# An adaLN transformer block on one core: chunk 1's queries and keys turned by transposing transfers instead of TensorE, with a new fixed order behind the first 150 ranks

## The chip, the core and the metric

The kernel runs on one core of a Trainium2 chip. A core has a tensor engine (PE, with its weight loads PEld shown apart), three engines for element-wise work (VectorE = DVE, ScalarE = ACT, GpSimd = POOL) and a queue engine (SyncE = SP) which here only issues transfers; ACT issues some too. Each engine works through its own list of instructions in order, and waits by semaphores for results of the others. The metric is the device time of one execution in microseconds (us); lower is better. Beside it there is a trace of one profiled execution, whose span runs from the first instruction to the last.

## The reference

One transformer block over S = 2048 tokens of width D = 640, all arrays bf16. The six modulation rows come from `silu(c) @ w_mod`.

```python
h = layernorm(x) * (1 + ca) + sa
q, k, v = split_heads(h @ wqkv)          # 32 heads of 20
scores = q @ k.T * 20 ** -0.5            # mask: 0 <= i - j < 256
x = x + ga * ((softmax(scores) @ v) @ wo)
h = layernorm(x) * (1 + cb) + sb
x = x + gb * ((sigmoid(h @ w_gate) * (h @ w_up)) @ w_down)    # F = 1536
```

A query attends to itself and the 255 tokens before it, so a stretch of 256 queries needs only its own keys and those of the stretch before.

## The kernel before

**Tiling.** The tokens are cut into 8 chunks of 256, each of two blocks of 128. For every chunk the program goes through these stages:

1. Layer norm of the two blocks (statistics on DVE and POOL, `ln_stats`), then turning the normalized rows to hT (D on partitions). For chunks 0 to 2 (`NPH = 3`) PE does this with an identity matrix (`pe_transposes`); later chunks use transposing transfers, `transp_dma` (L801 to L803), followed by the modulation on DVE, ACT or POOL (`modulate`).
2. Projections to Q, K and V (`qkv`, L902), chains of five matmuls L668 of 320 columns in chunk 0 and 480 afterwards, each into one of the four PSUM tiles of pool `p_M`. ACT or DVE copy them out (`evac`, L893 for ACT, L894 for DVE): V into its own tile, Q and K into staging tiles `stg`, in which each head of 20 columns gets 32.
3. Turning Q and K so that the head's columns lie on partitions. This is the place of the change. There are two ways, and `a < NPQ` (L937; a is the chunk) chooses. Either PE does it: two groups (`half`) of four 128x128 matmuls with the identity, M<-ident,stg, into a `p_M` tile, and a copy of 128x512 to QT or KT by ACT or DVE (operations named `qtr` and `evqt`). Or SP issues one transposing transfer of the block from `stg` to QT or KT (`qkt`). Before, `NPQ = 2`, so chunks 0 and 1 go by PE, the rest by transfers.
4. Scores in sets (`score_set`, L669, matmuls of 20 partitions, S<-QT,KT), all into the one large PSUM tile of `p_S`; exp on ACT (L1015, E<-S), which empties it; the masks by POOL selects (L1040). Each half of the heads (q = 0, 1) then has one burst of probability-times-V matmuls (`burst`, L1053, M<-E,V, named `pvs`) into two `p_M` tiles.
5. Normalization on DVE (`norm`): two transposes of 128x512 (L1082), a reciprocal, a multiplication (L1089), a transpose (L1091). The result is written to DRAM (doc) and read back as oT.
6. The output projection with wo and the residual addition, layer norm 2, its transposing transfers and modulation to h2T.
7. The MLP (`mlp`, L1195): gate and up matmuls with wg and wu, 128x256 each, a tanh on ACT (L1209), a product on DVE (L1211, hh), and the down matmuls with wd, followed by the residual addition on DVE (L1230) and the store of the output. The last block of the last chunk is split into columns 320, 192 and 128.

**What sets the order.** The program is first written as a list of some 2,100 operations (`Prog.op`), with their dependences. `PRIO` gives for each operation, in the order of its creation, one number: rank times five plus the number of the engine (PE, ACT, DVE, POOL, SP). `Prog.schedule` goes through the operations by this rank, puts each at the end of its engine's list, and gives PSUM and SBUF tiles their slots; there is no choice of order at run time. The list thus fixes which engine does an operation that several can do (copies, modulations, masks, stores), what precedes what on each engine, and in which order SP issues its transfers.

The one thing before that `schedule` also did was to go through a model of the time (durations, PE's change of mode, a queue of transfers, a port shared by DVE and POOL), only to choose among free slots of a pool the one whose last user was modelled to end first.

In the order before, the first scores of chunk 1 start at 37.23 us, the first MLP matmuls of chunk 0 at 76.8, and chunk 1's first burst at 54.85.

Of the kernel before, what the change touches and what calls it, by code (L numbers as in the profile page):

```python
# [25 lines left out]
SWITCH = 0.095  # L26
ENGATTR = {"pe": "tensor", "act": "scalar", "dve": "vector", "pool": "gpsimd", "sp": "sync"}
ENGS = ("pe", "act", "dve", "pool", "sp")
OVERLAP = {"pe": 0.0, "act": 0.085, "dve": 0.075, "pool": 0.045, "sp": 0.0}
# [52 lines left out]
class Prog:  # L82
# [69 lines left out]
    def schedule(self):  # L152


        free = {e: START for e in ENGS}
        bw = 0.0
        lastturn = False
# [3 lines left out]
        rr = 0  # L161
        pemode = 0
        portend = 0.0
# [16 lines left out]
        for o in sorted(self.ops, key=lambda x: x.prio):  # L180
# [4 lines left out]
            st = max([o.tmin, free[e] + (SWITCH if e == "pe" and o.mode != pemode else 0.0)]  # L185
                     + [d.end + (0.0 if d.eng == "pe" and e == "pe" else d.lat) for d in o.deps])
            if o.isdma and e == "sp":
                st = max(st, bw - QMAX)
            for t in o.tiles:
                if t.slot is None:  # L190
                    step = 1 if t.mate is None else 2
                    best = None
                    for s in range(0, len(t.pool.tenant), step):
                        rts = [slot_time(t.pool, s + k) for k in range(step)]
                        if None not in rts and (best is None or max(rts) < best[0]):
                            best = (max(rts), s)
# [6 lines left out]
                for x in t.prev:  # L203
                    st = max(st, x.end + x.lat)
            if e == "dve" and o.port:
                st = max(st, free["pool"])
            elif e == "pool":
                st = max(st, portend)
            o.start = st
            if e == "pe":  # L210
                pemode = o.mout
            dur = o.dur[e]
            free[e] = st + dur - OVERLAP[e]
            if e == "dve" and o.port:
                portend = free[e]
            if o.isdma:
                turn = o.dlat > 3.0
                if e == "sp" and bw - st > 2.0:
                    free[e] += 0.35 if o.dur[e] > 1.0 else 0.1
                bw = max(st + o.dlat, bw + (MIXED if turn != lastturn and bw > st + o.dlat else 0.0)) + o.work  # L220
                lastturn = turn
                o.end = max(bw - 0.83, st + dur)
                s = rr
                rr = (rr + 1) % NDMA
                dmacnt[s] += 16
                o.key, o.val = f"d{s}", dmacnt[s]
                if dmalast[s] is not None:
                    o.deps.append(dmalast[s])
                dmalast[s] = o
            else:  # L230
                o.end = st + dur
            order[e].append(o)
            o.done = True
            for t in o.tiles:
                t.left -= 1
                if t.left == 0:
                    last = {}
                    for x in t.ops:
                        if x.isdma:
                            last[x] = x  # L240
                    for e2 in ENGS:
                        xs = [x for x in t.ops if x.eng == e2 and not x.isdma]
                        if xs:
                            last[e2] = max(xs, key=lambda x: x.start)
                    t.rel = list(last.values())
                    freed[t] = max(x.end + x.lat for x in t.rel)
        self.order = order
        self.span = max(o.end for o in self.ops)
# [88 lines left out]
def c_pe(n):  # L337
# [3 lines left out]
PE_EPS = 0.14  # L341
PRIO = [
# [117 lines left out]
]  # L460
TR1 = 2
NPH = 3
NPQ = 2
PQ = ()
KEEP = 3
DSAFE = 1.5
# [840 lines left out]
```

## Time and profile before

| | |
|---|---|
| median of 3 runs | 326.33 us (325.88 to 327.26) |
| span of the profiled execution | 324.3 us |
| granted clock of TensorE | 1.000 |
| PE busy | 317.3 us, 98% |
| ACT, DVE, POOL busy | 212.3, 211.8, 187.2 us |
| moved by DMA | 37.85 MB |

The profile gives no time of its own for the profiled execution beside the span; the median of the runs is 2.0 us above that span. In the trace's rows, a group of instructions is written as engine, line, operation, out<-in and shape, with its count. Idle time of an engine stands in brackets with the engine or transfer that ended it. PE's matmuls overlap with their successors, so the length of one (about 0.4 us from issue to end) is more than the time by which it holds PE; that is read from one start to the next.

### The profile page before, as it was taken

Reading aid. Unit: us, or ns where it says so; the run is one execution under the profiler, and the core shown is the slowest. Engines: PE = TensorE matmul, PEld = TensorE weight load, DVE = VectorE, ACT = ScalarE, POOL = GpSimd, SP = SyncE. Lnnn points to the kernel's source line nnn. Section 1 sums busy time; section 2 is a strip of 40 time slices with the busy share of each in tenths; the row PEclk is TensorE's granted clock in tenths of the full one; section 3 lists DMA queues with packets and bytes.
Section 4 is the critical chain, followed back from the end, with each engine's and each line's share of the span. In section 5 each row is a group of like instructions: output and inputs, shape, how many; then the busy total and the mean of one; then the engine's idle time right before and its main releaser. Section 6 shows DMA issues by size and latency. Waiting matters only on the chain.

```text
span 324.3 us, 11594 instructions
## 1 busy us (share of the span) xinstructions
PE 317.3 (98%) x4872; PEld 222.7 (69%) x4873; DVE 211.8 (65%) x424; ACT 212.3 (65%) x316; POOL 187.2 (58%) x276
## 2 busy tenths in 40 slices
PE   8999999989999999999999999999999999999997
PEld 3564545446776568765776467877786788787885
DVE  5797898778687959674477475837463769264332
ACT  1899985889876687788687867786767764011120
POOL 5128869976668694847585939382939691012100
DMA  7998799989891383824405394340213032202101
GB/s 249 371 333 299 165 269 180 200 137 183 260 164 22 83 109 77 152 61 101 85 22 82 97 103 110 92 69 5 81 40 88 3 79 53 76 20 64 40 2 40
DMA packets 71694, 37.85 MB, mean 117 GB/s; under 512 B 45274, under 2 KB 70362, under 8 KB 71642
## 3 DMA queue, kind: packets, MB, share of 16 engines
q1 hardware_dynamic: 69616, 35.31, 48.3%
q10 hardware_dynamic: 2026, 1.80, 2.1%
q8 instruction: 38, 0.62, 0.8%
q14 instruction: 14, 0.11, 0.1%
HBM read 21.30 MB, written 5.25 MB: 82 GB/s over the span
## 4 chain that ended last, share of the span: by engine, by line
PE 73%; DMA 2%; SPq 2%; DVE 1%; POOL 1%; issue 0%; DVEq 0%
PE M L668 61%; PE S L669 6%; PE M L669 5%; DMA gbc<-gate 2%; SPq L803 2%; DVE wd L1192 1%; POOL x L793 0%; POOL st L788 0%; DVE hh L1211 0%; POOL E L1040 0%; DVE x L1230 0%; DVEq L310 0%
## 5 line engine op out<-in xcount | busy, mean ns | idle before, releaser
L1040 POOL TENSOR_SCALAR_AFFINE_SELECT E<-E 128x512 bf16<-128x512 bf16 (+1 forms) x176 | 142.6, 836 | 68.7 <-ACT E L1015 67.0
L1015 ACT ACTIVATE E<-S 128x512 bf16<-128x512 f32 (+2 forms) x184 | 150.9, 878 | 47.4 <-PE S L669 46.5
L668 PE MATMUL M<-wqkv,hT 128*128 128x480 bf16 (+1 forms) x340 | 73.9, 355 | 0.6 <-ACT hT L846 0.5
L668 PE MATMUL M<-h2T,wu 128*128 128x256 bf16 x480 | 68.0, 273 | 0.5 <-DVE hh L1211 0.5
L668 PE MATMUL M<-h2T,wg 128*128 128x256 bf16 x480 | 67.8, 273 | 0.0
L668 PE MATMUL M<-wd,hh 128*128 128x320 bf16 (+2 forms) x396 | 58.1, 295 | 0.0
L1209 ACT ACTIVATE sig<-M 128x512 f32<-128x512 f32 x48 | 28.9, 602 | 44.1 <-PE M L668 41.7
L1211 DVE SCALAR_TENSOR_TENSOR hh<-sig,M 128x512 bf16<-128x512 f32 x48 | 32.4, 681 | 37.1 <-ACT sig L1209 24.0
L668 PEld LDWEIGHTS M<-h2T,wu 128*128 128x128 bf16 x480 | 45.9, 98 | 8.4 <-issue 1.2
L668 PEld LDWEIGHTS M<-h2T,wg 128*128 128x128 bf16 x480 | 45.7, 98 | 7.1
L668 PEld LDWEIGHTS M<-wqkv,hT 128*128 128x128 bf16 x340 | 30.1, 98 | 27.6 <-DMA wqkv<-in_A_wqkv_dram 1.6
L668 PEld LDWEIGHTS M<-wd,hh 128*128 128x128 bf16 x396 | 36.8, 98 | 14.3 <-DVE hh L1211 0.2
L669 PEld LDWEIGHTS S<-QT,KT 20*64 20x64 bf16 (+1 forms) x1856 | 19.9, 100 | 21.3 <-ACT E L1015 12.0
L1230 DVE TENSOR_TENSOR x<-M,x 128x320 bf16<-128x320 f32 (+2 forms) x33 | 15.6, 476 | 27.2 <-PE M L668 27.2
L669 PE MATMUL S<-QT,KT 20*64 20x256 bf16 (+5 forms) x1856 | 32.1, 228 | 1.2 <-ACT E L1015 1.2
L776 DVE BATCH_NORM_STATS2 st<-x 128x6 f32<-128x320 bf16 x64 | 28.6, 477 | 2.3 <-DMA x<-in_A_x_dram 1.9
L1082 DVE STREAM_TRANSPOSE T<-M 128x512 f32<-128x512 f32 x32 | 21.5, 698 | 9.2 <-PE S L669 8.0
L668 PE MATMUL M<-wo,oT 128*128 128x320 bf16 x160 | 25.4, 299 | 0.0
L669 PE MATMUL M<-E,V 128*32 128x128 bf16 (+1 forms) x960 | 22.8, 246 | 0.8 <-ACT E L1015 0.4
L781 POOL TENSOR_SCALAR st<-st 128x2 f32<-128x2 f32 x16 | 3.7, 234 | 33.8 <-DVE st L778 33.6
L669 PEld LDWEIGHTS M<-E,V 128*32 128x32 bf16 x960 | 19.2, 97 | 5.3 <-issue 2.9
L1091 DVE STREAM_TRANSPOSE On<-Tn 128x1024 bf16<-128x1024 bf16 x16 | 19.8, 1240 | 0.3
(77 smaller groups left out, 240.2 us busy)
## 6 DMA issues: line engine op xcount, KB each, us to landing
x<-in_A_x_dram SPq DMA_DIRECT2D x23, 160.0 KB, 2.3
doc<-On SPq DMA_DIRECT2D x56, 40.0 KB
wd<-in_B_w_down_dram SPq DMA_DIRECT2D x4, 480.0 KB
wd<-in_w_mod_dram SPq DMA_DIRECT2D x5, 320.0 KB
wqkv<-in_A_wqkv_dram SPq DMA_DIRECT2D x4, 400.0 KB
wu<-in_w_mod_dram SPq DMA_DIRECT2D x5, 320.0 KB
oT<-doc SPq DMA_DIRECT2D x8, 192.0 KB, 2.5
out_dram<-x SPq DMA_DIRECT2D x9, 160.0 KB
```

Of the source, the lines that this page charges most:

```text
L668: return e.matmul(o, l, r, start=st, stop=sp, skip_group_check=True)
L669: return e.matmul(o, l, r, start=st, stop=sp, tile_position=tp, skip_group_check=True)
L776: A("dve", lambda e, g, bi=bi, j=j: e.bn_stats(v(bi * 12 + j * 6, 6), src[bi].ap[:, j * 320:(j + 1) * 320]), 0.48, reads=[src[bi].r()], wr ...
L781: A("pool", lambda e, g: e.tensor_scalar(v(28, n), var(), EPS, None, op0=ALU.add), 0.2, reads=[st.r(("m", bi)) for bi in range(n)], writes ...
L803: return e.dma_start_transpose(dst(), src())
L1015: A("act", lambda e, eng: e.activation(dst(), src(), ACT.Exp, scale=SM_SCALE), c_act(n), reads=[Sp.r()], writes=[E.r(key)], prio=3, tag=f" ...
L1040: A("pool", lambda e, eng: e.affine_select(rows(dst), rows(src), pattern=[[0, 8], [sign, n]], compare_op=ALU.is_ge, fill=0.0, base=base, c ...
L1082: A("dve", lambda e, g, h=h: e.transpose(T1.ap[:, 512 * h:512 * h + 512], X[h].ap), 0.694, reads=[X[h].r()], writes=[T1.r(h)], prio=3.5, t ...
L1091: A("dve", lambda e, g: e.transpose(On.ap[:], Tn.ap[:]), 1.22, reads=[Tn.r()], writes=[On.r()], prio=4, tag=f"tr2_{a}")
L1209: A("act", lambda e, g, pg=pg, sg=sg: e.activation(sg.ap[:], pg.ap[:], ACT.Tanh, scale=0.5), c_act(512), reads=[pg.r()], writes=[sg.r()], ...
L1211: A("dve", lambda e, g, pu=pu, sg=sg, f0=f0: e.scalar_tensor_tensor(out=hh.ap[:, f0:f0 + 2, :], in0=sg.ap[:].rearrange("p (a b) -> p a b", ...
L1230: A("dve", lambda e, g, ps=ps, bi=bi, c0=c0, n=n: e.tensor_tensor(x1[bi].ap[:, c0:c0 + n], ps.ap[:, 0:n], x1[bi].ap[:, c0:c0 + n], op=ALU. ...
```

## The change

The core is one constant. With `NPQ = 1` chunk 1's four `stg` tiles (Q and K of two blocks) go by a transposing transfer each instead of by eight groups of four matmuls and eight copies. Chunk 0 stays with PE.

```diff
-NPQ = 2
+NPQ = 1
```

With that 16 operations go and 4 come (2,121 to 2,109 in all), and `PRIO` has new numbers. The first 150 ranks keep their operations and engines, apart from two single loads of w_mod columns that change places and one that goes later (SP's list; the other engines' work is the same up to there). Behind them the order is new: projections, score sets, bursts and MLP pieces of neighbouring chunks interleave differently, and 87 operations with a choice of engines change theirs (copies, modulations, masks, stores; POOL gives 18 to DVE and ACT and takes 10, and four output stores go from ACT's queue to SP's). The last chain on PE is no longer the 128 columns of the last block but the second 320 columns of the last chunk's first block. SP's four new transfers stand in the order KT and QT of the second block, QT and KT of the first, ahead of the transfers that turn chunk 3's rows.

`schedule` loses its model of the time. A free slot is chosen by rank: the one whose last user has the lowest rank.

```diff
-        def slot_time(pool, s):
+        def slot_rank(pool, s):
             ten = pool.tenant[s]
             if ten is None:
-                if not all(x.done for x in pool.init[s]):
-                    return None
-                return max([x.end + x.lat for x in pool.init[s]], default=0.0)
+                return -1 if all(x.done for x in pool.init[s]) else None
             return None if ten.left else freed[ten]
...
-        for o in sorted(self.ops, key=lambda x: x.prio):
+        for rank, o in enumerate(sorted(self.ops, key=lambda x: x.prio)):
...
-                        rts = [slot_time(t.pool, s + k) for k in range(step)]
-                        if None not in rts and (best is None or max(rts) < best[0]):
-                            best = (max(rts), s)
+                        ranks = [slot_rank(t.pool, s + k) for k in range(step)]
+                        if None not in ranks and (best is None or max(ranks) < best[0]):
+                            best = (max(ranks), s)
...
                 if t.left == 0:
+                    freed[t] = rank
```

Last, the two `p_M` tiles of a burst need to be neighbours only where one DVE transpose takes both, which it doesn't here (`TR1` is 2):

```diff
     def burst(a, q, Es):
 
         X = [Tile(p_M, f"O{a}_{q}x"), Tile(p_M, f"O{a}_{q}y")]
-        X[0].mate, X[1].mate = X[1], X[0]
+        if TR1 == 1:
+            X[0].mate, X[1].mate = X[1], X[0]
```

More of the change, by code (lines that the diff above doesn't have):

```diff
@@ L25 @@
 NDMA = 24
-SWITCH = 0.095
 ENGATTR = {"pe": "tensor", "act": "scalar", "dve": "vector", "pool": "gpsimd", "sp": "sync"}
 ENGS = ("pe", "act", "dve", "pool", "sp")
-OVERLAP = {"pe": 0.0, "act": 0.085, "dve": 0.075, "pool": 0.045, "sp": 0.0}
 class Res:
@@ L152, in schedule @@
     def schedule(self):
-        free = {e: START for e in ENGS}
-        bw = 0.0
-        lastturn = False
         order = {e: [] for e in ENGS}
@@ L184, in schedule @@
             o.eng = e
[L185 to L188, printed above, removed]
             for t in o.tiles:
@@ L202, in schedule @@
                         take(t.mate, best[1] + 1 - t.odd)
[L203 to L215, printed above, removed]
-            if o.isdma:
[L217 to L223, printed above, removed]
-                rr = (rr + 1) % NDMA
[L225 to L231, printed above, removed]
+            if o.isdma:
+                dmacnt[rr] += 16
+                o.key, o.val = f"d{rr}", dmacnt[rr]
+                if dmalast[rr] is not None:
+                    o.deps.append(dmalast[rr])
+                dmalast[rr] = o
+                rr = (rr + 1) % NDMA
             order[e].append(o)
@@ L236, in schedule @@
                 if t.left == 0:
+                    freed[t] = rank
                     last = {}
[L238 to L244, printed above, removed]
+                    for x in sorted(t.ops, key=lambda x: x.prio):
+                        last[x if x.isdma else x.eng] = x
                     t.rel = list(last.values())
-                    freed[t] = max(x.end + x.lat for x in t.rel)
         self.order = order
-        self.span = max(o.end for o in self.ops)
     def emit(self):
@@ L466 @@
 DSAFE = 1.5
-START = 0.8
-PORTLAG = 0.05
-MIXED = 0.55
 NPB = 0
@@ L484 @@
 WSE = (("dve", "pool"), ("dve", "pool"))
-QMAX = 4.5
 WDT = 72.0
```

3 lines of the change are left out of this document (removed), and 229 rows, old and new, of the table PRIO.

## The prediction

> **What bounds the kernel now.** I read the page's shares of busy time first, then a table of windows that end where TensorE (PE) last waited, then its waits, then the timeline around them.
>
> ```profile
> span 324.3 us, 11594 instructions
> PE 317.3 (98%) x4872; PEld 222.7 (69%) x4873; DVE 211.8 (65%) x424; ACT 212.3 (65%) x316; POOL 187.2 (58%) x276
> PE 73%; DMA 2%; SPq 2%; DVE 1%; POOL 1%; issue 0%; DVEq 0%
> ```
>
> ```profile
> 18.34:37.23 18.89, 18.88 (x244) 11.08 (x240) 16.60 (x38) 16.87 (x30) 12.42 (x18) 1.00 0.81 258
> 37.23:54.85 17.62, 17.10 (x253) 8.24 (x251) 16.00 (x35) 14.38 (x21) 14.39 (x23) 1.00 1.04 222
> 54.85:70.48 15.63, 14.06 (x249) 7.57 (x248) 11.98 (x28) 12.65 (x20) 13.79 (x21) 1.00 1.03 182
> 70.48:86.54 16.06, 15.55 (x282) 11.06 (x283) 12.62 (x23) 13.99 (x23) 11.09 (x14) 1.00 1.01 219
> 86.54:270.02 183.48, 183.46 (x3253) 132.74 (x3254) 119.14 (x225) 135.74 (x191) 125.83 (x169) 1.00 0.41 80
> 270.02:324.30 54.28, 51.89 (x448) 42.86 (x446) 23.73 (x44) 8.45 (x15) 3.65 (x7) 1.00 0.14 40
> ```
>
> The chain that ended last is three quarters PE. The columns of the table are the window, its length, the busy time of PE, PEld, DVE, ACT and POOL, PE's granted clock, DMA share and GB/s. From 86.54 to 270.02 PE works 183.46 of 183.48 us, and in the last window it is idle only in the 2.4 us after its last matmul. So behind 86.54 an order can win nothing: only fewer matmuls or a shorter end count. Between 18.34 and 86.54 PE idles 0.01 + 0.52 + 1.57 + 0.51 = 2.6 us. There no other engine is full either; DVE comes nearest, with 16.00 of 17.62 (91%) in the second window.
>
> ```profile
> 40.48 2.20 PE L668 MATMUL M<-wqkv,hT 128*128 128x480 bf16 x10
> 42.65 0.41 PE L669 MATMUL S<-QT,KT 20*128 20x64 bf16 x32
> ...
> 64.13 0.43 PE L669 MATMUL S<-QT,KT 20*64 20x256 bf16 x24 [0.30 <-ACT E L1015]
> 64.66 2.82 PE L668 MATMUL M<-wqkv,hT 128*128 128x480 bf16 x12
> 67.91 0.43 PE L669 MATMUL S<-QT,KT 20*64 20x256 bf16 x24 [0.42 <-ACT E L1015]
> 68.26 1.79 PE L668 MATMUL M<-wqkv,hT 128*128 128x480 bf16 x8
> 70.48 1.50 PE L669 MATMUL M<-E,V 128*32 128x128 bf16 x64 [0.42 <-ACT E L1015]
> 86.54 1.14 PE L668 MATMUL M<-h2T,wu 128*128 128x256 bf16 x9 [0.51 <-DVE hh L1211]
> ```
>
> The idle column understates a stall. From 40.48 to 42.65 ten projection matmuls pass undisturbed in 2.17 us, 0.217 each. Twelve should take 2.60; from 64.66 to 67.91 they take 3.25, so 0.65 is lost where the column shows 0.42. Measured so, start to start against undisturbed stretches of the same shapes, I find 4.5 us lost between 18.34 and 90, 2.1 of them between 60 and 70.5. Both the score sets and the PV bursts in these rows wait for exps (L1015): a score set may start only when the set before it has left the one PSUM tile p_S.
>
> **The change part by part.**
>
> 1. Eight groups of four transposing matmuls on PE go (chunk 1's Q and K, two blocks, two halves).
>
> ```profile
> 28.18 0.58 PE L668 MATMUL M<-wqkv,hT 128*128 128x480 bf16 x2
> 28.59 0.39 PE L668 MATMUL M<-ident,stg 128*128 128x128 bf16 x4
> 28.82 0.77 PE L668 MATMUL M<-wqkv,hT 128*128 128x480 bf16 x3
> ```
>
> From 28.59 to 28.82 a group holds PE for 0.23 us, so the eight hold it 1.8. They stand before 60 us, in the stretch with stalls, so this is a gain only as far as PE is held by its own work there. All 1.8 at best, nothing if an exp's end sets the time anyway; I take 1.8 and price the stalls in step 3. Nothing else of PE's work changes in number: the rest of the count is equal.
>
> 2. Their evictions go, and four transposing transfers come.
>
> ```profile
> L893 ACT ACTIVATE QT<-M 128x512 bf16<-128x512 f32 x5 | 3.1, 614 | 0.3 <-PE M L668 0.3
> L894 DVE CAST QT<-M 128x512 bf16<-128x512 f32 x3 | 2.1, 686 | 1.1 <-PE M L668 1.1
> L803 SPq DMA_TRANSPOSE KT<-stg x12: 1237/1324/4257, 44.0 to 210.9; - x12
> L803 SPq DMA_TRANSPOSE QT<-stg x12: 1232/1278/2719, 45.6 to 191.2; - x12
> ...
> DMA to landing us min/median/max: 4.0/4.9/5.8
> ```
>
> Six evictions of 0.61 on ACT (3.7 us) and two of 0.69 on DVE (1.4) go, and eight times the wait for a p_M slot. SP issues four transfers more, about 1.3 us each, 5.2 together (17.0 if each takes the longest of its row, 4.26). In the new order they stand in front of hT3's two transfers, the wm2 loads and the gate's transfers; those are used by chunk 3's projections and by the MLP, more than 10 us later, so 5.2 us costs nothing there. At 17 it would reach the chunk 3 projections. By the order the last of the four can go when its staging tile is filled, about 31.3, and SP is free, about 32.0. With the row's 4.0 to 5.8 us it lands at 36.0 to 37.8. PE's program reaches chunk 1's first scores at about 36 (37.23 before), so it costs 0 to 1.8; I take 0.9, the median landing.
>
> The rule that speaks against this: the Trainium skill, "VectorE: DVE Perf Modes", in its section on the three transpose paths, gives 390 ns for a 128x128 bf16 transpose on TensorE and 1309 ns by the DMA crossbar, and advises TensorE wherever PSUM will do as destination. By it a transfer of eight blocks is an estimated 10.5 us and the four in series 42. The trace disagrees on both: eight blocks land within 4.0 to 5.8 us of issue, and four blocks on PE hold it 0.23 us.
>
> 3. The rest of the order is new: the score sets of chunks 1 and 2 start earlier against the projections, eight small jobs leave POOL (modulations, masks, LN applications), ACT loses most, DVE gains. Summing the durations in the new order ahead of chunk 2's second score set (74.44 before, row below) gives PE 47.8 (50.8 before), DVE 47.8 (45.5), ACT 42.0 (46.7), POOL 42.6 (44.8).
>
> ```profile
> L1015 ACT ACTIVATE E<-S 128x512 bf16<-128x512 f32 x120 | 67.3, 602 | 29.4 <-PE S L669 29.0
> ```
> ```profile
> 54.85 0.85 PE L669 MATMUL M<-E,V 128*32 128x128 bf16 x32
> ...
> 74.44 0.41 PE L669 MATMUL S<-QT,KT 20*128 20x64 bf16 x32
> ```
>
> Walking through the new order with these durations, I get: the first chunk-1 score set at about 36.5; the fourth held about 0.9 us by four exps of 0.60 in a row; first PV burst of chunk 1 about 51.5 to 52 (54.85 before); its second about 67 (70.48); chunk 2's second set 71.1 to 72. Some of each lead is only PE work moved behind the point. The stalls by 90 us add up to 3.4 with the first scores on time and 4.2 with them 0.9 late. I take 3.7 against 4.5: -0.8. Ends: 1.0 (the exps of the new order find p_S free earlier throughout) and 7.6 (DVE sets the pace, below).
>
> 4. The end. In the old order the last chain is the narrow one:
>
> ```profile
> 320.62 0.49 DVE L1230 TENSOR_TENSOR x<-M,x 128x320 bf16<-128x320 f32 x1 [1.47 <-PE M L668]
> 321.95 0.29 DVE L1230 TENSOR_TENSOR x<-M,x 128x128 bf16<-128x128 f32 x1 [0.31 <-PE M L668]
> ```
> ```profile
> x<-in_A_x_dram SPq DMA_DIRECT2D x23, 160.0 KB, 2.3
> out_dram<-x SPq DMA_DIRECT2D x1, 48.0 KB, 1.5
> ```
>
> In the new one PE ends with the first block's second 320 columns, followed by an addition of 0.49 instead of 0.29 and a store of the whole 160 KB. The addition costs 0.2; the store between 0 and 0.8 (2.3 for a 160 KB load against 1.5), I take 0.3: together +0.5.
>
> Four of the output stores move from ACT to SP and two x loads exchange queues late in the run; both queues have room in the fifth window (DMA share 0.41), so nothing, or 0.4 us of PE if an x arrives late. X tiles of a burst are no longer adjacent, which with two separate transposes (L1082) changes no instruction; 0.
>
> **Sum.** The profile gives the execution's span, 324.3; the median of the three runs (326.33, from 325.88 to 327.26) is 2.0 above it, and I take these 2.0 as what lies around the span in either kernel. 324.3 + 2.0 = 326.3; 326.3 - 1.8 (PE work) - 0.8 (stalls) + 0.5 (end) = 324.2.
>
> **The rivals.**
>
> *The order gains more.* Stalls fall to about 1.5: 326.3 - 1.8 - 3.0 + 0.5 = 322.0, with 1.0 and no cost at the end 321.0. For it: ACT and POOL have 4.7 and 2.2 us less to do by 74 us. Against: the single p_S remains, and the four-exp groups with it.
>
> ```profile
> PE S L669 <- ACT E L1015: 1.2, 4, 0.4
> ```
>
> *PE's saved work becomes idle.* If the exps set the pace up to 70 us, the 1.8 us are waited out: stalls 5 to 6.5, 325.0 to 326.5. For it: the longest list of PE's waits in this stretch is on L1015 (the row above). Against: they come to 1.2 us by that column, and ACT is only 81 to 89% busy in those windows.
>
> *DVE becomes the bound (the other side).* 47.8 us of DVE from 18.34 until chunk 2's second set: at 91%, the best window above, it takes 52.5 us and fits the walk. At 85.5%, its mean over the first three windows (44.58 of 52.14), it takes 55.9, 3.1 more, and the time is 324.2 + 3.1 = 327.3; at 84% 328.3. It decides from 87% down, where the 2.1 us gained are spent. For it: DVE carries evictions of projections, turned O and modulations on which PE's slots depend. Against: part of its 85.5% was waiting for PE.
>
> *The transfers come late (also slower).* If the four are issued at the longest in the row and land at 5.8, the last lands at 32.0 + 4.3 + 5.8 = 42.1 instead of 36.9, and since PE's order is fixed all 5.2 count: 329.4. It decides where the landing comes after 39, 7 us behind the issue. For it: DMA share 1.04 at 37 to 55 us, and wm loads in the same window. Against: twelve such transfers never took over 5.8. The skill's advice for TensorE points this way, though by its own figure the time would be far longer.
>
> **How the numbers follow.** A measurement here tells about 0.5% from no change (1.6 us: 324.7 to 328.0). Chances: the forecast, 323.3 to 325.1, 0.38 (0.28 of it under 324.7); the larger gain 0.20; idle instead of work 0.17; DVE 0.17 (half under 328.0); late transfers 0.08 (all slower). Faster 0.28 + 0.20 = 0.48, slower 0.08 + 0.08 = 0.16, same the other 0.36. The range from 321.0 to 328.3 leaves out the late transfers and the tail of the DVE case, and a little below. The forecast's own range is 323.3 to 325.1.
>
> **What would show it.** Right: 32 matmuls M<-ident,stg fewer; QT and KT transfers x14 each on SP, the first ones landing before PE's first 64-row score set, which starts at 36 to 38 without a wait for QT or KT; PE's lost time by 90 us about 3.7; PE gapless behind; a DVE addition 128x320 as the last one. Wrong: a wait of PE on stg's turned tiles, DVE over 90% busy in 40 to 75 us with waits <-DVE in PE's list, or PE idle behind 90 us, which no step here foresees.

## The result, and the profile after

The changed kernel takes 328.63 us (median of 6 runs, 327.27 to 330.03) where the kernel before took 326.11 beside it (6 runs, 325.86 to 327.26): ratio 1.0075, 95% interval 1.0055 to 1.0096. It is 2.5 us slower; 324.2 had been forecast. (The ratios here and below leave disturbed executions out, the medians do not; the two differ by up to 0.13 per cent.) The times also spread more: 2.8 us from lowest to highest, against 1.4.

The page of the kernel after, its span, its shares and its chain:

```profile
span 327.0 us, 11522 instructions
PE 315.2 (96%) x4840; PEld 220.3 (67%) x4841; DVE 210.4 (64%) x424; ACT 213.4 (65%) x316; POOL 181.0 (55%) x268
PE 81%; DVE 3%; DMA 1%; ACT 1%; issue 1%; ACTq 0%; DVEq 0%
```

PE has the 32 matmuls less and 2.1 us less to do. The windows of the kernel after, same columns as before (window, length, busy time of PE, PEld, DVE, ACT, POOL, granted clock, DMA share, GB/s):

```profile
18.34:37.23 18.89, 17.70 (x207) 9.57 (x205) 17.70 (x40) 15.09 (x26) 12.02 (x16) 1.00 1.01 276
37.23:54.85 17.62, 14.97 (x273) 7.21 (x277) 14.64 (x33) 12.59 (x17) 13.01 (x18) 1.00 0.98 223
54.85:70.48 15.63, 14.82 (x246) 7.87 (x234) 13.05 (x28) 12.24 (x18) 12.72 (x17) 1.00 1.00 207
70.48:90.00 19.52, 19.36 (x359) 13.60 (x360) 13.24 (x26) 16.58 (x27) 14.21 (x21) 1.00 0.90 190
90.00:270.02 180.02, 179.24 (x3125) 129.25 (x3114) 116.27 (x224) 135.89 (x191) 116.29 (x156) 1.00 0.39 81
270.02:327.00 56.98, 54.03 (x517) 44.51 (x514) 24.34 (x45) 11.72 (x21) 6.53 (x11) 1.00 0.16 43
```

PE is idle 1.2 us in the first window (0.0 before) and 2.65 in the second (0.5 before); the third is better than before (0.8 against 1.6). Neither DVE nor ACT is full in the second: 14.64 and 12.59 of 17.62. Counted as in the prediction, start to start against undisturbed stretches, PE loses 8.0 us from 18 to 100 us, where it lost 4.5. That fits the end of its list: the last matmul ends at 324.06 us instead of 321.93, 2.1 us later with 1.8 us less to do. What PE waited for, in the list of the kernel after (engine, line, releaser: us in total, times, longest):

```profile
PE S L622 <- ACT E L968: 1.9, 4, 0.7
PE S L621 <- DMA wd<-in_w_mod_dram: 1.5, 2, 1.2
PE M L621 <- DVE stg L847: 1.0, 1, 1.0
PE M L621 <- DVE x L1118: 0.8, 1, 0.8
PE M L621 <- DVE hh L1165: 0.8, 1, 0.8
PE S L622 <- DMA KT<-stg: 0.4, 1, 0.4
```

Line numbers are lower by 46 or 47 here; L622 are the score and burst matmuls, L968 the exps, L1118 the residual addition. The turned keys themselves (KT<-stg) cost 0.4 us. PE's timeline of the kernel after where most is lost:

```profile
37.26 0.43 PE L622 MATMUL S<-QT,KT 20*64 20x256 bf16 x24 [0.41 <-DMA KT<-stg]
...
44.93 0.43 PE L622 MATMUL S<-QT,KT 20*64 20x256 bf16 x24 [0.69 <-ACT E L968]
45.29 1.19 PE L621 MATMUL M<-wqkv,hT 128*128 128x480 bf16 x5
47.44 1.17 PE L621 MATMUL M<-wqkv,hT 128*128 128x480 bf16 x5 [0.96 <-DVE stg L847]
49.35 0.43 PE L622 MATMUL S<-QT,KT 20*64 20x256 bf16 x24 [0.74 <-ACT E L968]
...
54.45 1.50 PE L622 MATMUL M<-E,V 128*32 128x128 bf16 x64
...
70.75 1.50 PE L622 MATMUL M<-E,V 128*32 128x128 bf16 x64
...
75.35 0.41 PE L622 MATMUL S<-QT,KT 20*128 20x64 bf16 x32
```

The last three lines are chunk 1's two bursts and chunk 2's second score set, which stood at 54.85, 70.48 and 74.44 before. The waits at 47.44 and 49.35 lead back through two engines. DVE's timeline of the kernel after:

```profile
40.67 0.35 DVE L765 TENSOR_SCALAR hT<-hT,mA 128x256 bf16<-128x256 bf16 x1 [1.17 <-DMA hT<-x]
40.94 1.31 DVE L1036 STREAM_TRANSPOSE T<-M 128x512 f32<-128x512 f32 x2
...
44.18 0.63 DVE L847 CAST stg<-M 128x480 bf16<-128x480 f32 x1
44.74 1.23 DVE L1045 STREAM_TRANSPOSE On<-Tn 128x1024 bf16<-128x1024 bf16 x1
```

and ACT's:

```profile
42.81 2.06 ACT L968 ACTIVATE E<-S 128x512 bf16<-128x512 f32 x4 [0.55 <-PE S L622]
46.00 1.26 ACTq L523 DMA_DIRECT2D doc<-On  x2
47.36 0.60 ACT L968 ACTIVATE E<-S 128x512 bf16<-128x512 f32 x1 [2.48 <-DVE stg L847]
```

DVE's next instruction after 39.50 is a modulation of chunk 3's rows, whose transfer lands 1.17 us later (40.58; in the kernel before the two landed at 34.3 and 35.6). Behind it stands the turning of O, so O (On) is ready at 45.97. ACT is done with four exps at 44.88, but two stores of O come next in its list; it stands until 46.00, issues them until 47.26, and only then begins the exps of a score set that PE had ready at 45.4.

The start of that: SP's timeline of the kernel after.

```profile
22.32 0.95 SPq L523 DMA_DIRECT2D wo<-in_A_wo_dram  x1
23.30 1.33 SPq L523 DMA_DIRECT2D wu<-in_w_mod_dram  x2
26.44 2.29 SPq L756 DMA_TRANSPOSE KT<-stg  x1
28.84 4.29 SPq L756 DMA_TRANSPOSE QT<-stg  x2
33.23 1.26 SPq L756 DMA_TRANSPOSE KT<-stg  x1
34.62 3.75 SPq L756 DMA_TRANSPOSE hT<-x  x2
```

The first added transfer, issued at 26.44, lands at 32.99, 6.55 us later and right behind the last weight load (32.00); the first two hold SP for 2.29 and 2.93 us. Chunk 3's two transfers (hT<-x) are issued 3 us later than before and take 5.2 and 4.5 us instead of 2.7 and 2.6. The later issue is not the four transfers' alone. SP is free of them at 34.50, but the first of chunk 3's two also has to wait for the projection that still reads the old rows, and in the new order that projection ends at 34.53; in the kernel before, the last thing it waited for was POOL's normalized rows, at 31.61.

### The profile page after: what moved, and what is told of

Read it like the earlier page. It is cut to its first block, busy times and chain, and to the rows that moved or that the text cites. A ratio compares the mean times of both kernels' runs of the same rounds, so it can differ in the third digit from the quotient of the medians.

```text
span 327.0 us, 11522 instructions
## 1 busy us (share of the span) xinstructions
PE 315.2 (96%) x4840; PEld 220.3 (67%) x4841; DVE 210.4 (64%) x424; ACT 213.4 (65%) x316; POOL 181.0 (55%) x268
## 4 chain that ended last, share of the span: by engine, by line
PE 81%; DVE 3%; DMA 1%; ACT 1%; issue 1%; ACTq 0%; DVEq 0%
PE M L621 68%; PE S L622 7%; PE M L622 6%; DMA hT<-x 1%; ACT E L968 1%; DVE T L1036 1%; ACTq L523 0%; DVE On L1045 0%; DVE Tn L1043 0%; DVE x L749 0%; DVE stg L847 0%; DVE hh L1165 0%; DVE x L1184 0%; DVE x L1118 0%; DVE Dr L1041 0%
## 5 line engine op out<-in xcount | busy, mean ns | idle before, releaser
L968 ACT ACTIVATE E<-S 128x512 bf16<-128x512 f32 (+2 forms) x184 | 150.1, 877 | 49.5 <-PE S L622 45.5
L621 PE MATMUL M<-h2T,wu 128*128 128x256 bf16 x480 | 69.6, 273 | 0.0
L621 PE MATMUL M<-h2T,wg 128*128 128x256 bf16 x480 | 68.9, 273 | 0.0
L622 PEld LDWEIGHTS S<-QT,KT 20*64 20x64 bf16 (+1 forms) x1856 | 20.0, 100 | 22.4 <-ACT E L968 11.2
L622 PE MATMUL S<-QT,KT 20*64 20x256 bf16 (+5 forms) x1856 | 32.2, 228 | 2.3 <-ACT E L968 1.9
L621 PE MATMUL M<-wo,oT 128*128 128x320 bf16 x160 | 26.7, 300 | 0.8 <-DVE hh L1165 0.8
L622 PE MATMUL M<-E,V 128*32 128x128 bf16 (+1 forms) x960 | 22.7, 246 | 0.1
L622 PEld LDWEIGHTS M<-E,V 128*32 128x32 bf16 x960 | 19.0, 97 | 4.7 <-issue 2.8
L1118 DVE TENSOR_TENSOR x<-M,x 128x320 bf16<-128x320 f32 x32 | 15.3, 484 | 9.1 <-PE M L621 8.4
```

The lines of the kernel that those rows point to most:

```text
L621: return e.matmul(o, l, r, start=st, stop=sp, skip_group_check=True)
L622: return e.matmul(o, l, r, start=st, stop=sp, tile_position=tp, skip_group_check=True)
L968: A("act", lambda e, eng: e.activation(dst(), src(), ACT.Exp, scale=SM_SCALE), c_act(n), reads=[Sp.r()], writes=[E.r(key)], prio=3, tag=f" ...
L1118: A("dve", lambda e, g, ps=ps, bi=bi, half=half: e.tensor_tensor(x1[bi].ap[:, half * 320:half * 320 + 320], ps.ap[:, 0:320], x1[bi].ap[:, ...
```

## The experiments

Two theories to begin with. A: the loss is the new order's, by stores of O that stand in ACT's list ahead of exps. B: it is the four transfers', by what they delay.

### The constant alone, in the old order

```diff
 (order of before, NPQ = 1)
 PE:  - 8 x four matmuls M<-ident,stg        ACT, DVE:  - 8 copies 128x512
 SP:  + qkt1 KT(b1), QT(b0), then hT3's two, then KT(b0), QT(b1)
```

> The constant alone: the order of before, with chunk 1's eight turning groups and eight copies taken out and the four transposing transfers put on SP at the first place where their staging tiles are full; nothing else moves. Theory A (the lost time of the changed kernel comes from its new order: ACT's queue holds stores of O that wait for DVE, with exps behind them): this kernel does not have that, PE loses 1.8 us of work, and the first chunk-1 scores start at about 37; 325 to 326.5 us. Rival B (the transposing transfers themselves cost: they hold SP, land late and push chunk 3's turned rows and the loads behind them): the first chunk-1 scores or the chunk 3 modulations come 1 us or more later than before, 327.5 us or more.

Measured: 332.25 us (5 runs) against 325.85, ratio 1.0195 (1.0178 to 1.0212). PE stands 4.5 us at 35.5 to 40.0 for the last turned tile: the last two were issued only behind chunk 3's, at 35.27 and 36.58. That much was a poor place. So once more with all four ahead of chunk 3's:

> The constant alone in the old order once more, now with SP issuing the four transposing transfers as soon as their tiles are full, all ahead of chunk 3's two; in the run before, the third and fourth stood behind those and were issued at 35.27 and 36.58, and PE waited 4.5 us for the last, that landed at 39.80. If SP's order was the cost: the last is issued at about 33.5 and lands at 37 to 38, PE's wait falls to 1.5 to 2.5 us; 329 to 330.5 us. If the old order stalls for other reasons without the turning on PE (chunk 3's rows late, up to 40): 331 us or more.

Measured: 329.99 us (4 runs) against 325.78, ratio 1.0124 (1.0085 to 1.0162). The last lands at 37.18, PE waits 1.5 us for it; but chunk 3's rows now land at 39.65 and 40.15, and PE loses 3.1 us between 37 and 43 (0.5 in the kernel before). The constant without a new order loses 6.4 and 4.2 us in these two kernels, with 1.8 us of matmuls gone: theory A alone is not enough. Not all of that is waiting: in every run of the two TensorE's granted clock is below 1.000 on the mean, which the next section takes up.

### The four transfers alone

The kernel before, all its matmuls and copies kept, with four transfers added that send chunk 1's staging tiles into buffers that chunk 2 overwrites later. The output is the same.

```diff
+                if a == 1:
+                    old[key, bi] = s
+                if a == 2:
+                    transp_dma(QT/KT of chunk 2, old[key, bi], ..., "qkd1")   # ranks: ahead of hT3's two
                 if a < NPQ or (a, key, bi) in PQ:
```

> The kernel before, unchanged on PE, ACT, DVE and POOL, with four transposing transfers more on SP: chunk 1's staging tiles are also sent into the buffers of chunk 2's Q and K, where they are overwritten later, at the places of the old order with the transfers first (chunk 3's two behind them). It measures what the four transfers cost by their place in SP's queue alone. Theory D (in-order queues: chunk 3's rows land at about 40 instead of 34.3 and 35.6, and DVE and ACT wait with other work behind): PE loses 2.5 to 3.5 us between 37 and 43, as it did in the old order with transfers, without the 1.7 us wait for the turned tiles: 328 to 329.5 us. Rival (the transfers are hidden, and those losses came from the copies and matmuls taken out of an order tuned for them): 325.6 to 326.6 us.

Measured: 330.02 us (4 runs) against 325.94, ratio 1.0113 (1.0090 to 1.0136). Nothing but four transfers was added, and 4.1 us are lost by the medians. ACT's timeline of the kernel before at this place, then of this kernel:

```profile
37.44 0.59 ACT L811 ACTIVATE hT<-hT,mA 128x256 bf16<-128x256 bf16 x1
37.93 1.92 ACT L1015 ACTIVATE E<-S 128x1536 bf16<-128x1536 f32 x2
```
```profile
40.58 0.60 ACT L811 ACTIVATE hT<-hT,mA 128x256 bf16<-128x256 bf16 x1 [2.77 <-DMA hT<-x]
41.09 1.92 ACT L1020 ACTIVATE E<-S 128x1536 bf16<-128x1536 f32 x2
```

In the kernel before, the modulation of chunk 3's rows finds them there, with 1.8 us to spare (35.64 to 37.44). Now they land at 40.50, ACT stands 2.77 us, and the exps of chunk 1's first set come 3.2 us later. DVE is held at the same time by a gate transfer that had also been pushed back:

```profile
41.65 0.32 DVE L710 TENSOR_SCALAR gq<-M 128x160 bf16<-128x160 f32 x1 [2.84 <-DMA gate<-gq]
```

Two variants ask what of the four does it: their place, or that they transpose.

> The kernel before with the same four transposing transfers added, but issued later: behind chunk 3's two, the first gate transfer and two x loads, at about 37 to 42 us. If the place in SP's queue made the cost (4.1 us when they stood ahead of chunk 3's): chunk 3's rows land at 34 to 36 again, ACT's and DVE's waits of 2.8 us at 38 to 41 are gone, and 0 to 1.5 us is left for what stands behind them now; 326 to 327.5 us. If their traffic made it, wherever they stand: 329 us or more.

```diff
 SP:  hT3's two, x9, gate, x8,
+     the four transfers,
      wu, gate's broadcast, x11, wg, x10, ...
```

Measured: 332.60 us (4 runs) against 325.81, ratio 1.0209 (1.0190 to 1.0229): worse. Chunk 3's rows land at 34.32 and 35.64 as before, and the waits for them are gone, as expected. But now the gate's broadcast stands behind the four; it lands at 49.76 (41.83 before). DVE's timeline of this kernel:

```profile
42.20 0.80 DVE L1094 TENSOR_TENSOR Tn<-T,Dr 128x640 bf16<-128x640 f32 x1
49.85 0.49 DVE L1258 TENSOR_TENSOR wo<-wo,gbc 128x640 bf16<-128x640 bf16 x1 [6.85 <-DMA gbc<-gate]
```

The expectation saw one victim and overlooked the next in the queue.

> As the first kernel of this kind (the four ahead of chunk 3's two transposing transfers), but the four are plain copies of the same 256 KB blocks. If the length of a transposing transfer and its issue make the cost (it holds SP 1.3 to 4.7 us each there): plain ones hold SP about 0.45 each, chunk 3's rows land at 35 to 37, 326 to 327.5 us. If any four transfers of this size at this place do it (the queue still holds the weight loads until 32): chunk 3's rows land at 38 or later, 328 us or more.

```diff
-                    transp_dma(dst, old[key, bi], ...)
+                    dma(dst, old[key, bi], ...)          # same bytes, same place
```

Measured: 327.80 us (4 runs) against 325.81, ratio 1.0060 (1.0038 to 1.0083). Plain copies cost 2.0 us where transposing ones cost 4.1, by the medians. They hold SP 0.74, 1.01, 2.33 and 0.59 us, chunk 3's rows land at 38.49 and 39.11. The landings are those of the second half of the expectation; the time lies between the two halves.

The medians hide one more thing. PE's timeline of the kernel with the transposing transfers ahead of chunk 3's, and a window of it (columns as before, the granted clock is the 0.50):

```profile
43.05 0.43 PE L669 MATMUL S<-QT,KT 20*64 20x256 bf16 x24 [2.58 <-ACT E L1020]
43.41 3.58 PE L668 MATMUL M<-wqkv,hT 128*128 128x480 bf16 x10
44.06:47.48 3.42, 3.42 (x41) 1.30 (x39) 2.71 (x7) 1.93 (x3) 0.66 (x1) 0.50 0.92 229
```

and the same place with plain copies:

```profile
41.67 0.43 PE L669 MATMUL S<-QT,KT 20*64 20x256 bf16 x24 [1.69 <-ACT E L1020]
42.03 2.20 PE L668 MATMUL M<-wqkv,hT 128*128 128x480 bf16 x10
```

Behind a wait of 2.58 us TensorE is granted half its clock for 3.42 us, and the ten projections take 3.58 us instead of 2.20. That costs PE up to 1.7 us and lowers the mean clock of the run by 0.005 (half of 3.42 in 328). The kernel with transposing transfers has a mean clock of 0.994 or 0.995 in three of its four runs (330.02, 330.02 and 330.27 us) and of 1.000 in the fourth, 328.70; the four runs with plain copies are all at 1.000, from 326.93 to 328.91. So at the full clock transposing transfers cost 2.8 us, by a single run, and plain ones 2.0. That transposing is half of the price is not shown. The transposing transfers landed no later behind their issue (4.4 to 7.0 us; plain 4.8 to 7.0), but held SP for 7.7 us in all instead of 4.7, and chunk 3's last rows landed 1.4 us later.

The kernels with the constant alone are at 0.985 to 0.990 and 0.990 to 0.995 in their runs, the one with the late transfers at 0.990 to 0.995: one to three such stretches, or up to 1.7 to 5 us of their losses of 6.4, 4.2 and 6.8. The changed kernel is not among them: five of its six runs are at 1.000, and the one at 0.995 is its longest, 330.03. Nor is the next one, whose four runs are all at 1.000.

### The turning back on TensorE, in the new order

> The new order with chunk 1 turned on TensorE again: the four transfers are out, eight groups of four matmuls and eight copies (engines as before) stand a few ranks behind the copies that they need. Theory A: the wait of ACT for O stays, 1.8 us of PE work and eight copies come on top; the first chunk-1 scores 1 to 2 us later than 37.3; 329.5 to 332 us. Rival B: chunk 3's turned rows land 3 us or more earlier than 40.6, DVE and ACT do not wait, 326 to 328 us in spite of the work.

```diff
 (order of after, NPQ = 2)
 SP:  - the four qkt1
 PE:  + 8 x four matmuls M<-ident,stg, each a few ranks behind its copy
 ACT, DVE:  + 8 copies 128x512, on the engines that they had before
```

Measured: 329.11 us (4 runs) against 325.85, ratio 1.0098 (1.0081 to 1.0115), beside 1.0075 for the changed kernel: the intervals overlap. By theory A it should have been 329.5 to 332, by B 326 to 328. Chunk 3's rows land at 40.69 and 41.51 even so, since their transfers must wait for the last projection that reads the old ones, and that ends at 36.99 instead of 34.53, with the added matmuls ahead of it. So in the new order the transfers neither gain nor cost a clear amount against TensorE, and the new order with TensorE's turning is slower than the old one with it by 3.3 us. The order does not become good by taking the transfers out; that it was made for them cannot be separated from it here. With the later edits in the order (below) the same exchange was made again:

> The same order with chunk 1 turned on TensorE (eight groups of matmuls and eight copies in place of the four transfers, as in the earlier kernel of that kind). If the transfers are worth it once nothing waits behind them, this one is slower than the one with transfers by PE's 1.8 us or more: 326.5 to 329 us. If the transfers delay chunk 3's rows by as much as they save (the rival): the same to 0.5 us.

Measured: 329.53 us (4 runs) against 325.94, ratio 1.0114 (1.0096 to 1.0132); the kernel with the same order and the transfers took 326.88 beside it. There the kernel with the transfers is 2.6 us faster, more than PE's 1.8 us of matmuls. The places of the eight groups were not varied, and chunk 3's last rows land at 41.40 with them and at 40.15 with the transfers; how much of the 2.6 us is that, is not shown.

### The waits in the new order, one by one

> The changed kernel with four stores moved: the second half's O of chunk 0 goes to DRAM from SP's queue at the same ranks, not from ACT's. Theory A: in the changed kernel ACT is done with four exps at 44.88, waits for O until 45.97, issues two stores until 47.26, and the fourth set's exps start at 47.36, though their scores were there at 45.4. Without the stores these exps start at 45.4; the next score set starts at 47.3 instead of 49.35; 326.3 to 326.9 us. Rival B: ACT gets the 2 us back in another wait, or the next set waits for masks or projections as long; 328 to 329 us. Rival C (DVE is the bound up to 75 us): the score set moves but the gain is gone by 70 us, 328 us.

```diff
-OWE = lambda a: "act" if a == 0 else "sp"
+OWE = lambda a: ("act", "sp") if a == 0 else "sp"    # four stores of O, second half: act -> sp, same ranks
```

Measured: 329.23 us (4 runs) against 325.85, ratio 1.0099 (1.0076 to 1.0123): no gain. PE's timeline of this kernel:

```profile
35.54 0.57 PE L621 MATMUL M<-wqkv,hT 128*128 128x480 bf16 x2
38.01 0.43 PE L622 MATMUL S<-QT,KT 20*64 20x256 bf16 x24 [1.91 <-DMA KT<-stg]
...
46.04 2.25 PE L621 MATMUL M<-wqkv,hT 128*128 128x480 bf16 x10
48.22 0.43 PE L622 MATMUL S<-QT,KT 20*64 20x256 bf16 x24
```

The two waits at 47 and 49 us are gone, as theory A had it (1.9 us). In this execution 1.5 us of it were lost ten microseconds earlier, at a place that the edit does not touch: the last turned tile took 4.99 us from issue to landing (3.99 in the changed kernel). Whether the median lost its gain in the same way is not shown; the four runs lie within 1.6 us.

> The changed kernel with two of DVE's instructions moved: its two modulations of chunk 3's rows, which wait for transfers that land at 40.58, stand behind the turning and dividing of O instead of in front. In the changed kernel DVE is idle from 39.50 to 40.67 for that landing, with the turning of O behind it. Theory A: O is ready at about 44.9 instead of 45.97, ACT's stores are issued at 44.9 to 46.2, the fourth set's exps start at 46.3; 1.0 to 1.2 us gained, 327.4 to 327.7 us. If the length of the wait on ACT is set by something else than DVE's chain (the issue of a store itself), less than 0.4 us.

```diff
 DVE:  - modulate hT3 (two), turn O, divide, turn O back
       + turn O, divide, turn O back, modulate hT3 (two)
```

Measured: 327.84 us (4 runs) against 325.85, ratio 1.0053 (1.0038 to 1.0068): 0.8 us under the changed kernel's by the medians, where 1.0 to 1.2 had been expected; the intervals of the two ratios overlap (1.0055 to 1.0096 there), so a gain is likely and not shown. Both together:

> Both of the earlier edits in one kernel: the four stores of O on SP's queue, and DVE's modulations of chunk 3 behind the turning of O. If the stores on ACT and DVE's wait were the cause of the lost time between 43 and 49 us, the stalls there fall from 2.7 us to under 0.8, and what is left to explain is the wait for the turned tiles at 36 us: 326.5 to 328.5 us, by when the last of them lands (4.0 to 5.0 us after its issue in the two runs so far). If the pace is set elsewhere (exps and DVE up to 75 us), 328.5 to 329.5 us, as with the stores alone.

Measured: 327.88 us (4 runs) against 325.78, ratio 1.0053 (1.0032 to 1.0074). The stalls between 43 and 49 us did not fall: DVE's copies are late (1.1 us) behind others.

A third theory, D, asks why the transfers land late: that they queue behind the loads issued before them.

> The changed kernel with one transfer moved on SP: the 800 KB load of wo (issued at 22.3, landing at 30.1, first used after 50) stands behind chunk 3's transposing transfers. Theory D (the transposing transfers queue behind the loads issued before them: in the changed kernel the first is issued at 26.44 and lands at 32.99, right behind the last wm1 load at 32.00): the loads end about 2.3 us earlier (wo's own landing minus the one before, 30.12 - 27.80), the first two turned tiles land about 2 us earlier, the fourth 0.5 to 1, chunk 3's rows at about 38 to 39; the first score set does not wait, DVE's idle 1.17 us at 39.5 shrinks; 327.2 to 328.0 us. Rival (the transfers' own length, with one block pair after the other, sets the landings): landings as before to 0.3 us, 328.3 to 328.9 us.

```diff
 SP:  - wo, wm1, wm1, qkt1 x4, hT3 x2, wm2
      + wm1, wm1, qkt1 x4, hT3 x2, wo, wm2
```

Measured: 328.13 us (10 runs, 326.52 to 331.36) against 325.78, ratio 1.0085 (1.0055 to 1.0115). Theory D's landings came true for the turned tiles: the first lands at 31.30 instead of 32.99, the last at 35.62 instead of 37.22, and the first set does not wait. Chunk 3's rows did not come at 38 to 39 but at 39.39 and 39.96: SP was free for them at 33.67 and stood until 33.99 for the projection that reads the old rows. And the load now ahead of wm2 makes that one late, 45.21 instead of 42.47. PE's waits of this kernel:

```profile
PE M L622 <- DMA hh<-in_w_mod_dram: 2.5, 1, 2.5
PE S L622 <- issue: 1.2, 1, 1.2
```

Then all edits in one: stores, turns, wo late, one modulation of chunk 4 behind a residual addition, one scaling of wd behind an MLP product, and the end of PE's list as before.

> The changed kernel with all the waits found so far taken out by place: stores of O on SP, chunk 3's modulations behind the turning of O, wo's load late, on DVE chunk 4's modulation behind the residual addition (its transfer lands at 64.55, PE loses 0.97 at 65), one scaling of wd behind a product of the MLP (PE loses 0.92 at 97), and the end of PE's list as in the kernel before (0.5). Summed: 1.9 + 0.5 + 1.0 + 0.9 + 0.5 = 4.8, 323.8 us. If a stall that is taken away comes back as another, since DVE or the exps set the pace, 326 to 328 us.

Measured: 326.77 us (10 runs, 325.60 to 328.45) against 325.78, ratio 1.0030 (1.0013 to 1.0047). 1.9 us better than the changed kernel by the medians, 1.5 by the ratios, where 4.8 had been summed. PE's waits show 1.6 us for wm2 again. Three kernels tried to place wo's load better: behind wm2 as well, behind the three x loads, or where the changed kernel has it.

> All edits once more, with wo's load behind the last load of w_mod too, and two of ACT's modulations of chunk 4 behind one exp. In the run with all edits PE waited 1.6 us at 44.0 for that w_mod load, which landed at 43.97 behind wo's, and 1.0 us at 66.85 for exps that stood behind modulations waiting for a transfer that landed at 63.80. Without these: 326.77 - 1.6 - 0.5 = 324.7 us, under the 325.8 of the kernel before. If each wait that is taken away comes back elsewhere: 326 us or more.

Measured: 326.88 us (12 runs, 325.96 to 328.78) against 325.94, ratio 1.0028 (1.0011 to 1.0044). The wait for wm2 is gone and another stands there. DVE's timeline of this kernel, then PE's list:

```profile
44.85 0.48 DVE L729 BATCH_NORM_STATS2 st<-x 128x6 f32<-128x320 bf16 x1
47.36 0.49 DVE L729 BATCH_NORM_STATS2 st<-x 128x6 f32<-128x320 bf16 x1 [2.04 <-DMA x<-in_A_x_dram]
47.77 0.64 DVE L847 CAST stg<-M 128x480 bf16<-128x480 f32 x1
```
```profile
PE M L621 <- DVE stg L847: 2.8, 1, 2.8
```

> All edits in the new order, with wo's load behind the three x loads, since in the last kernel of the kind DVE was idle 2.04 us for an x load that landed behind wo's, with copies behind it, and PE waited 2.8 us for one of them. Without that wait: 326.88 - 2.8 + 0.3 = 324.4 us; if the wait appears at a third place of the same stretch (36 to 56 us), 326 us or more, and the stretch has no room for that load.

Measured: 327.43 us (12 runs, 326.08 to 330.23) against 325.81, ratio 1.0051 (1.0031 to 1.0071). PE waits 1.5 us for DVE's copies at 46.9 and loses 2.0 at 67 to 69, where chunk 4's rows land at 66.24 (64.55 in the changed kernel).

> All edits in the new order except that wo's load stays where the changed kernel has it; the three kernels with that load moved each got a wait for another load of 1.5 to 2.8 us in its place. Against the kernel with the stores and turns edited alone (327.9): 0.9 (the scaling of wd) and 0.5 (the end) and up to 0.9 (chunk 4's modulations) less: 325.6 to 326.5 us. If the waits between 44 and 52 us, 3.1 us in that kernel, vary with the landings: any value from 325 to 328.

Measured: 329.19 us (4 runs, 328.06 to 330.42) against 325.76, ratio 1.0102 (1.0076 to 1.0128): not better than the changed kernel, and 2.4 us over the same edits with wo's load moved. Its profiled execution, 326.3 in span, is shorter than the changed kernel's, but it is the shortest of the four runs. The mean clocks of the four are 1.000, 1.000, 0.995 and 0.990, which explains a part: at the full clock it took 328.06 and 328.93, the kernel with all edits 325.60 to 327.30.

### The same kind of edit in the kernel before

> The kernel before, with no transfer added, and the same kind of edit that the study suggests: an instruction that waits is put behind what others wait for. On DVE three scalings of wd, behind a gate transfer that lands at 83.06, go behind the MLP product for which PE waits at 85.65 to 86.54 (0.68 lost); one of ACT's four modulations of chunk 4, that hold up exps at 64 to 66, goes to DVE (about 0.5). If both waits go: 325.8 - 1.2 = 324.6 us, faster than both kernels. If they are replaced by the next one: 325.4 to 326 us.

```diff
 DVE:  - scale wd (four), MLP product 2, product 3
       + scale wd (one), MLP product 2, scale wd (three), product 3
 ACT -> DVE:  one modulation of chunk 4
```

Measured: 326.02 us (12 runs) against 325.76, ratio 1.0008 (0.9998 to 1.0017): no difference. Both waits moved on, as PE's list of this kernel shows:

```profile
PE M L669 <- DVE stg L894: 0.7, 1, 0.7
PE M L669 <- DVE hh L1211: 0.5, 1, 0.5
```

The 0.68 us at 85.65 became 0.60 at 87.85, for the product behind the scalings. No kernel of the study beats the kernel before.

## Why the prediction was wrong, point by point

The term of the sum that failed is that of the stalls: 3.7 us were put in for the new order, and 8.0 measured. These 4.3 us are nearly the whole of the 4.4 between 324.2 and 328.63; the terms for PE's work and for the end held.

- **Step 1, PE's work** was right: 32 matmuls and 2.1 us of busy time less (forecast 1.8).
- **Step 2, the transfers**, put at nothing what was not nothing. "those are used by chunk 3's projections and by the MLP, more than 10 us later, so 5.2 us costs nothing there" looked at the last reader and not at the first. The first are modulations of chunk 3's rows on ACT and DVE, 1.8 us behind the landing in the kernel before, and since these engines work in order, everything behind them waits too. The same four transfers, added alone, cost 4.1 us, 1.7 of it at half the clock in the profiled run. In the changed kernel chunk 3's rows land about 5 us later than before. Of that 3 us are their later issue, for which the projection at 34.53 would have been enough, and the rest is the longer way to the landing; putting the turning back on TensorE did not bring them earlier, and the new order was no faster for it (329.11). So the four transfers' share of the 8.0 us is not separated from the order's.
- **Step 2, the landing of the last turned tile**, was right: 37.22 (36.0 to 37.8), and the wait for it 0.4 us. The rival *the transfers come late* put its price there. The transfers did come late, but the bill came from what stood behind them.
- **Step 3, the stalls**: 3.7 us forecast, 8.0 measured by 100 us. The first scores of chunk 1 came at 37.26 (about 36.5 in the walk), its bursts at 54.45 and 70.75 (51.5 to 52 and 67), chunk 2's second set at 75.35 (71.1 to 72): the lead was gone by the first burst. The walk used durations, and took every transfer and every store as landed or issued in time. It passed over the two stores of O in ACT's list ahead of a set's exps, where ACT stood from 44.88 to 47.26. Two more waits lie far behind the four transfers: 0.97 us at 65 and 0.92 at 97, where a residual addition stands behind chunk 4's rows and an MLP product behind scalings of wd; the second lies behind 90 us, where no step foresaw any. The four exps in a row did cost about what was said: 0.7 by the column at 44.93.
- **Step 4, the end**: right. 2.95 us from PE's last matmul to the end instead of 2.39, +0.56 (forecast 0.5).
- **The rival DVE** did not come. DVE is 94% busy in the first window, but 83% in the second and third, and 87% from 18.34 to chunk 2's second set; there its longest waits are for turned rows of x (1.8 us) and for PE (1.6). That the rival's 328.3 lies close to the measurement is chance.
- **Readings that do not hold, whatever came.** The row "4.0/4.9/5.8" rests on two transfers, issued at 65.67 and 88.94 us, the only ones of QT and KT for which the view has a landing; "twelve such transfers never took over 5.8" is not in it, and behind the weight loads the first took 6.55. Each at the longest of its own row, the four issues come to 14.0 us (twice 4.26 and twice 2.72), not 17.0; SP was held 7.7, up to 2.93 for one. The rival of idle work left out the end's 0.5 us: its stalls of 5 to 6.5 give 325.5 to 327.0 by the sum. And the 2.0 us around the span are 1.7 to 1.8 in every run that shows both.
- **The rule of the Trainium skill** ("VectorE: DVE Perf Modes", Rules for kernel authors), that TensorE is to be taken where PSUM will do as destination, gave the right sign against this change in the old order, for another reason than its figures: no transfer of eight blocks took 10.5 us, the longest of the four here 6.55, and the price came from what stood behind them.

What stays open: how the 8.0 us divide between the four transfers and the order; why the kernel with all edits but wo's load measures 2.4 us above its neighbours, of which the clock explains a part; and how much of the new order's 3.3 us loss with the turning on TensorE would go if an order were searched for that.

## What to carry to other kernels

Before a transfer is called hidden, list what stands behind it in its queue and find for each the first instruction that waits for it, not the last; then what is queued behind that instruction on its engine. The DMA share of a window does not tell whether there is room: in the kernel before it is 0.42 from 32 to 34 us and 0.60 from 34 to 36, and four transfers ahead of chunk 3's two moved both of those landings by 5 us; behind them, they moved the gate's broadcast by 8. A fixed order is worth what its assumed landings are worth, so an order with no room between landing and first use should be timed over many runs and not from one profile. And a wait of PE can cost more than its own length: read the granted clock of every run beside its time before a loss is put down to a transfer.

## What the runs showed of the hardware

- Four transposing transfers of 256 KB blocks and four plain copies of the same blocks at the same place in the queue landed 4.4 to 7.0 and 4.8 to 7.0 us behind their issue, and held SP for 7.7 and 4.7 us. The Trainium skill ("Advanced Engine Details and Errata", X-Bar Transpose) has transposing transfers as fast as regular ones; the landings here agree, and SP's time for the issue differs.
- The granted clock of TensorE fell to half for 3.4 us behind waits of PE of 2.58 and 2.82 us, for 6.8 us from within one of 5.44, in one kernel right behind one of 1.07; behind one of 2.53 it did not fall. What decides it is not shown. One kernel's ten runs at a mean clock of 1.000 took 325.96 to 327.45 us, its two at 0.995 took 328.14 and 328.78.
- The time for which an issue holds SP is not constant: transposing issues took 1.31 and 1.21 us at 31.6 and 33.1 us in the kernel before and 4.26 at 73.6, the plain copies of the same blocks from 0.59 to 2.33. That the transfers still moving make the difference is an inference.
- The four kernels in the new order that ran ten or twelve times spread by 2.8 to 4.8 us (326.52 to 331.36 for one of them), the kernel before, measured beside that one, by 0.9 (325.35 to 326.20). Their longest runs are at a mean clock of 0.995 or below.
- In several kernels PE stood 0.6 to 1.2 us in the middle of a score set at 57 to 59 us with nothing in the trace that it waited for ("issue"); the cause is not shown.
